# Linear attention and a tanh-shrink MLP on one core: output weights loaded ahead of a query tensor, attention steps moved between matmul slices, activations by pairs of tiles

## The chip, the cores and the metric

One core of a Trainium2 chip. The metric is the device time of one launch in microseconds (us), on the slowest (here the only) core. Executions of this kernel agree within about 0.3%, which is 0.9 us; most runs were repeated and are compared with runs of the kernel before on the same chip in the same rounds.

## The reference

Attention without softmax, by a positive feature map phi, for 8 batches of 576 tokens and 8 heads of 64; its result feeds an MLP over all 4608 tokens. Inputs arrive as float32; the kernel multiplies in bfloat16.

```python
phi  = lambda x: np.where(x > 0, x, np.exp(x) - 1.0) + 1.0
q_p, k_p = phi(q), phi(k)                       # (8, 8, 576, 64)
kv  = np.einsum('bhsd,bhse->bhde', k_p, v)
z   = np.sum(k_p, axis=2)
num = np.einsum('bhsd,bhde->bhse', q_p, kv)
den = np.einsum('bhsd,bhd->bhs', q_p, z)[..., None] + 1e-06
x   = (num / den).transpose(0, 2, 1, 3).reshape(4608, 512)
h   = x @ w_in                                  # w_in  512 x 2048
out = (h - np.tanh(h)) @ w_out                  # w_out 2048 x 512
```

## The kernel before

The tokens go through the MLP in 9 chunks of 512. A chunk is layer 1 (16 tiles of 4 matmuls; each tile is one PSUM bank of 128 x 512, then tanh on ScalarE and a subtraction on VectorE, which writes `gT`) and layer 2 (16 steps of 4 matmuls, then an eviction and a store). A matmul of 512 columns takes 0.216 us at full pace, so a tile or a step takes 0.86 us. The attention of the next batch is put between these matmuls, at places given by the lists `s1` (after a tile of layer 1) and `s2` (after a step of layer 2). As a batch has 576 tokens and a chunk 512, chunk 1 holds the last 64 tokens of batch 0 and the first 448 of batch 1: it can't begin before batch 1's attention is done, and so on.

Chunk 0 is special. Its layer 2 runs while `w_out` is still being loaded, in four slices of 512 KB. So its 16 steps go by slices: steps 0 to 3 use slice 0, steps 4 to 7 slice 1, and so on. Between the steps stand, for batch 1: phi of q, the transposes of q (`a_qT_pe`), kv, the denominator (`a_den`), the numerators with their copy to SBUF by ScalarE (`num1`), and the "spread", a matmul that broadcasts the reciprocals over partitions, after which VectorE multiplies. Numerators and spread use the same four PSUM banks (4 to 7). In the recorded texts, "slice" stands both for a quarter of `w_out` and for what is called a step here.

In the lines of profiles below, PE is TensorE, DVE VectorE, ACT ScalarE, POOL GpSimd, and SPq and ACTq are the DMA issues of SP and ScalarE. TensorE's work has these lines in the kernel before / in the changed one: L367 / L366 layer 1, L382 / L387 layer 2, L165 / L164 transposes of q, L178 / L177 kv of batch 1, L200 / L199 kv of later batches, L277 / L276 denominator, L318 and L321 / L317 and L320 numerators, L355 / L354 spread.

```python
    def l1act(fi, h, gT):
        th = mpool.tile([128, 512], F32, name="th")
        nc.scalar.activation(th, h, AF.Tanh)
        nc.vector.tensor_sub(gT[:, fi, :], h, th)
    ...
    load_q(0); load_k(0); make_identity(nc, ident); load_v(0)
    for g in range(4):
        load_wi(g)
    load_k(1)
    load_wo(0)
    load_q(1)
    ...
    load_wo(1)
    load_v(1)
    load_wo(2)
    ...
            # c == 0
            s2[0].append(lambda: a_qphi(1, 0))
            s2[1].append(lambda: (a_qphi(1, 1), load_q(2), load_wo(3), load_k(2), load_v(2)))
            s2[4].append(lambda: a_qT_pe(1, 0, side))
            s2[5].append(lambda: a_qT_pe(1, 1, side))
            s2[5].append(lambda: (b0_scale_rest(side), prepare()))
            s2[6].append(lambda: a_kv(1, side))
            s2[8].append(lambda: a_den(1, side))
            s2[9].append(lambda: (num1(), a_split(1)))
            s2[11].append(lambda: (spread1(0), a_qphi(2, 0)))
            s2[13].append(lambda: (spread1(1), a_qphi(2, 1), a_qT_dma(2)))
            s2[15].append(lambda: (a_kphi(2, 0), a_vp(2, 0, nc.gpsimd), a_vp(2, 1, nc.gpsimd)))
        elif n1 < B:
            s1[6 if c == 1 else 5].append(lambda: a_kv_cols(n1, attn))
            s1[9 if c == 1 else 8].append(lambda: (a_den(n1, attn), a_spread(n1)))
```

From batch 2 on, `a_spread` broadcasts the reciprocals by DMA instead: four small stores to DRAM (`ds`), then, when these have landed, two loads of 576 KB that read them back to 64 partitions each (`rdb`). All loads are issued by GpSimd; stores and the broadcast by SP.

## Time and profile before

| | kernel before |
|---|---|
| time, median of 3 runs | 295.21 us (295.07 to 295.33) |
| span in the profile | 293.7 us |
| TensorE busy | 285.4 us, 97% |
| VectorE, ScalarE, GpSimd busy | 183.9, 150.6, 34.6 us |
| end of TensorE's last matmul | 289.69 us |

Two more are wanted for the comparison, from the page's groups of instructions of the kernel before (line, engine, operation, operands, shapes, count, then busy us, mean ns of one, then idle us before them and what ended it):

```profile
L373 DVE TENSOR_TENSOR gT<-ps_all,th 128x512 bf16<-128x512 f32 x144 | 96.5, 687 | 46.7 <-ACT th L372 46.0
L372 ACT ACTIVATE th<-ps_all 128x512 f32<-128x512 f32 x144 | 85.3, 597 | 48.1 <-PE ps_all L367 42.2
```

This is the work that the change merges in pairs: 144 subtractions and 144 tanh of one bank each. And the longest of TensorE's waits over the whole kernel before (us in total, times, longest):

```profile
PE ps_all L382 <- DMA w_out_sb<-in_moe_w_out_dram: 1.7, 1, 1.7
```

It is for the second slice of `w_out`, and the one that the change goes for.

### The profile page before, as it was taken

How to read it: one execution, taken by the hardware profiler on the slowest of the kernel's cores; microseconds unless marked ns; L12 is line 12 of the kernel's file. 1: busy time of each engine (PE TensorE's matmuls, PEld its weight loads, DVE VectorE, ACT ScalarE, POOL GpSimd, SP SyncE). 2: the span in 40 equal slices, each digit the busy share in tenths (PEclk: the TensorE clock that was granted, in tenths of full speed). 3: DMA queues.
4: the chain of work that ended last, by engine and by line, in shares of the span. 5: the costliest groups of instructions: out<-in, count | busy, mean ns of one | idle time of the engine just before them, and what ended most of it. 6: DMA issues, size and time to landing. Idle time of an engine off the chain costs nothing.

```text
span 293.7 us, 4685 instructions
## 1 busy us (share of the span) xinstructions
PE 285.4 (97%) x1801; PEld 134.1 (46%) x1801; DVE 183.9 (63%) x326; ACT 150.6 (51%) x233; POOL 34.6 (12%) x55
## 2 busy tenths in 40 slices
PE   8999799999999999999999999999999999999994
PEld 2544364444444444544444445444444444444443
DVE  4759857996578665775578557955780478008600
ACT  4948717766355654555356535752561166136411
POOL 8562030420030002000020003000000000000000
PEclk9999999999999999999999999999999999999998
DMA  7999999897969765957797769787117310130033
GB/s 104 193 205 214 206 206 211 178 186 151 215 119 208 154 142 117 192 120 173 149 152 147 179 138 144 120 203 143 38 34 167 71 37 0 41 85 19 2 71 71
DMA packets 38534, 38.95 MB, mean 133 GB/s; under 512 B 16304, under 2 KB 33264, under 8 KB 37744
## 3 DMA queue, kind: packets, MB, share of 16 engines
q0 software_dynamic: 17008, 18.35, 38.2%
q1 hardware_dynamic: 21424, 20.27, 30.9%
q8 instruction: 14, 0.23, 0.3%
q14 instruction: 8, 0.07, 0.1%
q10 hardware_dynamic: 80, 0.03, 0.0%
HBM read 43.91 MB, written 9.55 MB: 182 GB/s over the span
## 4 chain that ended last, share of the span: by engine, by line
PE 81%; DMA 9%; DVE 5%; POOL 3%; issue 1%; ACT 0%; DVEq 0%; POOLq 0%
PE ps_all L382 39%; PE ps_all L367 35%; DMA w_out_sb<-in_moe_w_out_dram 5%; DMA w_in_sb<-in_moe_w_in_dram 4%; PE ps_all L318 2%; PE ps_all L200 2%; DVE gT L373 1%; PE ps_all L575 1%; DVE xT L360 1%; PE ps_all L277 1%; DVE r L136 1%; DVE kp L137 1%; POOL v L409 1%; PE ps_all L178 1%; DVE qp L137 1%
## 5 line engine op out<-in xcount | busy, mean ns | idle before, releaser
L382 PE MATMUL ps_all<-w_out_sb,gT 128*128 128x512 bf16 x560 | 128.2, 379 | 1.7 <-DMA w_out_sb<-in_moe_w_out_dram 1.7
L367 PE MATMUL ps_all<-xT,w_in_sb 128*128 128x512 bf16 x576 | 128.1, 379 | 0.4 <-DMA w_in_sb<-in_moe_w_in_dram 0.4
L373 DVE TENSOR_TENSOR gT<-ps_all,th 128x512 bf16<-128x512 f32 x144 | 96.5, 687 | 46.7 <-ACT th L372 46.0
L372 ACT ACTIVATE th<-ps_all 128x512 f32<-128x512 f32 x144 | 85.3, 597 | 48.1 <-PE ps_all L367 42.2
L367 PEld LDWEIGHTS <-w_in_sb 128*128 128x128 bf16 x576 | 55.2, 98 | 66.8 <-issue 0.9
L382 PEld LDWEIGHTS <-gT 128*128 128x128 bf16 x560 | 53.9, 98 | 65.9 <-issue 2.1
L388 ACT COPY osb<-ps_all 128x512 f32<-128x512 f32 (+2 forms) x37 | 21.2, 574 | 76.5 <-PE ps_all L382 59.8
L329 DVE TENSOR_TENSOR xT<-ps_all,rdb 128x512 bf16<-128x512 f32 x24 | 16.5, 690 | 14.2 <-PE ps_all L318 14.2
L135 ACT ACTIVATE e<-qraw 128x1152 bf16<-128x1152 bf16 x16 | 18.5, 1163 | 4.6 <-DMA qraw<-in_q_dram 4.6
L137 DVE TENSOR_TENSOR kp<-e,r 128x1152 bf16<-128x1152 bf16 x15 | 12.1, 809 | 12.5 <-ACT e L135 11.6
L135 ACT ACTIVATE e<-kraw 128x1152 bf16<-128x1152 bf16 x15 | 17.4, 1163 | 0.2 <-DMA kraw<-in_k_dram 0.2
L137 DVE TENSOR_TENSOR qp<-e,r 128x1152 bf16<-128x1152 bf16 x16 | 12.1, 758 | 7.9 <-ACT e L135 7.1
L378 POOL COPY g<-gT 1x1 bf16<-1x1 bf16 x5 | 0.9, 179 | 108.4 <-DVE gT L373 108.4
L318 PE MATMUL ps_all<-qT,kz 128*128 128x512 bf16 x28 | 10.1, 379 | 0.0
L434 PE MATMUL ps_all<-zero 128*128 128x512 bf16 x29 | 8.8, 466 | 1.2 <-DVE zero L396 1.2
L136 DVE TENSOR_SCALAR r<-qraw 128x1152 bf16<-128x1152 bf16 x16 | 7.3, 455 | 1.9 <-DMA qraw<-in_q_dram 1.9
L200 PE MATMUL ps_all<-vp,kp 64*128 64x136 bf16 x216 | 7.6, 220 | 0.2 <-DVE kp L137 0.2
L136 DVE TENSOR_SCALAR r<-kraw 128x1152 bf16<-128x1152 bf16 x15 | 7.7, 514 | 0.0
L200 PEld LDWEIGHTS <-kp 64*128 64x128 bf16 x216 | 6.4, 94 | 2.9 <-issue 2.5
L286 DVE RECIPROCAL rden<-den 128x144 f32<-128x144 f32 x7 | 7.4, 1053 | 0.2
L93 POOL DMA_DIRECT2D qraw<-in_q_dram x7 | 5.2, 748 | 14.7 <-DVE r L136 12.3
L93 POOL DMA_DIRECT2D kraw<-in_k_dram x7 | 5.3, 752 | 4.3 <-issue 1.6
(80 smaller groups left out, 105.3 us busy)
## 6 DMA issues: line engine op xcount, KB each, us to landing
out_dram<-osb SPq DMA_DIRECT2D x70, 128.0 KB
rdb<-ds SPq DMA_DIRECT2D x12, 576.0 KB
kraw<-in_k_dram POOLq DMA_DIRECT2D x7, 576.0 KB, 5.9
qraw<-in_q_dram POOLq DMA_DIRECT2D x7, 576.0 KB, 8.0
v<-in_v_dram POOLq DMA_DIRECT2D x7, 576.0 KB, 10.8
w_in_sb<-in_moe_w_in_dram POOLq DMA_DIRECT2D x8, 256.0 KB, 11.7
w_out_sb<-in_moe_w_out_dram POOLq DMA_DIRECT2D x4, 512.0 KB, 14.3
qraw<-in_q_dram POOLq DMA_DIRECT2D x2, 288.0 KB, 4.4
```

The costliest lines, as they stand in the source:

```text
L93: nc.gpsimd.dma_start(out=t.rearrange("q h i j d -> q (h i) (j d)"), in_=x.rearrange("(n q) x -> q n x", n=4))
L135: return (lambda: nc.scalar.activation(e, x, AF.Exp), lambda: nc.vector.tensor_scalar(r, x, 0.0, 1.0, ALU.max, ALU.add), lambda: nc.vector ...
L136: lambda: nc.vector.tensor_scalar(r, x, 0.0, 1.0, ALU.max, ALU.add),
L137: lambda: nc.vector.tensor_tensor(y, e, r, ALU.min))
L200: nc.tensor.matmul(ps[hg][:, i, :], kp[r, i, j].rearrange("p h d -> p (h d)"), vp[r, i, j, :], start=(j == 0), stop=(j == J - 1))
L318: nc.tensor.matmul(ps, kz[:, p // 2, p % 2, 0:128], qT[:, p % 2, 0:8, p // 2, :], start=True, stop=True)
L329: nc.vector.tensor_mul(xT[:, p, S * b:S * b + 512].rearrange("p (j t c) -> p j t c", j=8, t=4), ps.rearrange("p j (t c) -> p j t c", t=4), ...
L367: nc.tensor.matmul(h, w_in_sb[:, 2 * (p % 2) + p // 2, fi * 128:(fi + 1) * 128], xT[:, p, c * 512:(c + 1) * 512], start=(n == 0), stop=(n ...
L372: nc.scalar.activation(th, h, AF.Tanh)
L373: nc.vector.tensor_sub(gT[:, fi, :], h, th)
L382: nc.tensor.matmul(o, gT[:, fi, i * 128:(i + 1) * 128], w_out_sb[:, fi, :], start=(fi == 0), stop=(fi == NF - 1))
L388: nc.scalar.copy(osb[:, f0:f1], o[:, f0:f1])
```

## The change

Its intent: load slice 1 of `w_out` ahead of q of batch 1, and slice 3 ahead of q of batch 2, so that layer 2 of chunk 0 never waits for weights; move what needs q of batch 1 behind step 7; hand the copy `vp` from GpSimd back to VectorE, which it slows; halve the number of activation instructions; spread the last stores over two queues. The core of the diff (cut: the loader of `w_in`, which now takes a size, renamed arguments, and the helper `q2`, whose first and last call a comment stands for):

```diff
-    mpool = ctx.enter_context(tc.tile_pool(name="mpool", bufs=3))
+    mpool = ctx.enter_context(tc.tile_pool(name="mpool", bufs=2))
...
+    def l1act2(fi, h, gT):
+        th = mpool.tile([128, 2, 512], F32, name="th")
+        nc.scalar.activation(th, h, AF.Tanh)
+        nc.vector.tensor_sub(gT[:, fi:fi + 2, :], h, th)
...
-    def gate(gT, fi):
-        nc.gpsimd.tensor_copy(g0, gT[0:1, fi, 0:1])
+    def gate(qT):
+        nc.gpsimd.tensor_copy(g0, qT[0:1, 1, J - 1, 1, 63:64])
...
-        nc.scalar.copy(osb[:, f0:f1], o[:, f0:f1])
+        if f0:
+            nc.vector.tensor_copy(osb[:, f0:f1], o[:, f0:f1])
+        else:
+            nc.scalar.copy(osb[:, f0:f1], o[:, f0:f1])
-        for half, q_ in enumerate((nc.sync, nc.sync if f1 < DM or c < NC - 1 or i < 3 else nc.scalar)):
+        last = c == NC - 1 and i == 3
+        for half in range(2):
-            q_.dma_start(...)
+            (nc.scalar if last and half else nc.sync).dma_start(...)
...
-    for g in range(4):
-        load_wi(g)
+    for f0, n in ((0, 256), (256, 256), (512, 512), (1024, 512), (1536, 512)):
+        load_wi(f0, n)
     load_k(1)
     load_wo(0)
+    load_wo(1)
     load_q(1)
...
-    load_wo(1)
     load_v(1)
     load_wo(2)
+    load_wo(3)
...
-            s2[0].append(lambda: a_qphi(1, 0))
-            s2[1].append(lambda: (a_qphi(1, 1), load_q(2), load_wo(3), load_k(2), load_v(2)))
-            s2[4].append(lambda: a_qT_pe(1, 0, side))
-            s2[5].append(lambda: a_qT_pe(1, 1, side))
-            s2[5].append(lambda: (b0_scale_rest(side), prepare()))
-            s2[6].append(lambda: a_kv(1, side))
-            s2[8].append(lambda: a_den(1, side))
-            s2[9].append(lambda: (num1(), a_split(1)))
-            s2[11].append(lambda: (spread1(0), a_qphi(2, 0)))
-            s2[13].append(lambda: (spread1(1), a_qphi(2, 1), a_qT_dma(2)))
-            s2[15].append(lambda: (a_kphi(2, 0), a_vp(2, 0, nc.gpsimd), a_vp(2, 1, nc.gpsimd)))
+            s2[3].append(lambda: a_qphi(1, 0))
+            s2[4].append(lambda: (a_qphi(1, 1), load_q(2), load_k(2), load_v(2)))
+            s2[0].append(prepare)
+            s2[7].append(lambda: (a_qT_pe(1, 0, side), a_qT_pe(1, 1, side), a_kv(1, side)))
+            s2[8].append(lambda: b0_scale_rest(side))
+            s2[9].append(lambda: a_den(1, side))
+            s2[10].append(lambda: (num1(), a_split(1)))
+            s2[11].append(lambda: spread1(0))
+            # phi of q of batch 2: its exps and maxima after steps 12 and 13, its minima after 14
+            s2[13].append(lambda: (spread1(1), q2(1)))
+            s2[15].append(lambda: a_kphi(2, 0))
         elif n1 < B:
-            s1[6 if c == 1 else 5].append(lambda: a_kv_cols(n1, attn))
-            s1[9 if c == 1 else 8].append(lambda: (a_den(n1, attn), a_spread(n1)))
+            s1[7 if c == 1 else 5].append(lambda: a_kv_cols(n1, attn))
+            s1[10 if c == 1 else 8].append(lambda: (a_den(n1, attn), a_spread(n1)))
         if c == 1:
             s1[1].append(lambda: a_kphi(2, 1))
+            for i in range(2):
+                s1[3].append(lambda i=i: a_vp(2, i))
...
-            l1act(fi, h, gT)
+            if c == 0:
+                l1act(fi, h, gT)
+            elif fi % 2:
+                n = dense.order[(dense.n - 1) % 6]
+                l1act2(fi - 1, ps_all[:, n - 1:n + 1, :], gT)
```

## The prediction

> **What bounds the kernel now.** I read the page first, then the chain of waits in order of time, then the timeline of TensorE over the first 63 us, then those of the other engines, and the landing time of each load. The page has PE busy 97% of a span of 293.7 us. Busy PE is no proof of a full PE, so I looked at the pace in the chain (start us, length us, what):
>
> ```profile
> 21.85 14.25 DMA w_out_sb<-in_moe_w_out_dram
> 36.10 0.04 issue
> 36.14 1.02 PE ps_all L382 x4
> ...
> 67.81 10.36 PE ps_all L382 x48
> ...
> 286.18 3.51 PE ps_all L575 x32
> ```
>
> 48 matmuls of 512 columns in 10.36 us are 0.216 us each, and this pace holds with no other engine in the chain from 62.5 us to 289.7 us. One chunk there (128 such matmuls and the attention ones between) takes 30.36 us (82.61 to 112.96, 112.96 to 143.32, ...). The change removes no matmul. So time can come only from before 62.5 us and from the tail. The timeline of PE shows what is lost there (brackets: idle before, and what ended it):
>
> ```profile
> 30.82 3.62 PE L382 MATMUL ps_all<-w_out_sb,gT 128*128 128x512 bf16 x16
> 36.14 1.02 PE L382 MATMUL ps_all<-w_out_sb,gT 128*128 128x512 bf16 x4 [1.70 <-DMA w_out_sb<-in_moe_w_out_dram]
> ...
> 41.54 1.90 PE L382 MATMUL ps_all<-w_out_sb,gT 128*128 128x512 bf16 x8
> ...
> 44.61 0.28 PE L321 MATMUL ps_all<-qT,kz 128*128 128x64 bf16 x4
> ...
> 47.41 0.30 PE L355 MATMUL ps_all<-w,sel 32*128 32x144 bf16 x8
> ...
> 58.47 0.71 PE L200 MATMUL ps_all<-vp,kp 64*128 64x136 bf16 x18 [0.17 <-DVE kp L137]
> 59.11 2.76 PE L367 MATMUL ps_all<-xT,w_in_sb 128*128 128x512 bf16 x12
> 61.81 0.72 PE L277 MATMUL ps_all<-qT,kz 128*32 128x144 bf16 x16
> 62.46 1.90 PE L367 MATMUL ps_all<-xT,w_in_sb 128*128 128x512 bf16 x8
> ```
>
> The 16 matmuls at 30.82 need 3.45 us, so 36.14 - 34.27 = 1.87 us are lost to the second slice of w_out. In chunk 1, L200 takes 1.5 us instead of 1.17 and L277 0.65 instead of 0.36: some 0.7 us lost to a late VectorE. Two more views matter. ScalarE copies the numerators of batch 1, and VectorE is slow while GpSimd copies vp (52.6 to 55.4):
>
> ```profile
> 44.92 0.37 ACT L347 COPY ns<-ps_all 128x256 f32<-128x256 f32 x1 [5.38 <-PE ps_all L321]
> 45.20 2.06 ACT L345 COPY ns<-ps_all 128x512 f32<-128x512 f32 x4
> ```
> ```profile
> 52.97 1.40 DVE L136 TENSOR_SCALAR r<-kraw 128x1152 bf16<-128x1152 bf16 x1
> 54.48 1.51 DVE L137 TENSOR_TENSOR kp<-e,r 128x1152 bf16<-128x1152 bf16 x1
> ```
>
> The copies end at 47.26, and L355, which writes over all four banks they read, starts at 47.41: already only 0.1 us of slack. The tail is in the DMA queues of SP and ACT:
>
> ```profile
> 290.53 0.55 SPq L392 DMA_DIRECT2D out_dram<-osb  x1
> ```
> ```profile
> 290.01 0.56 ACTq L392 DMA_DIRECT2D out_dram<-osb  x1
> ```
>
> **What the Trainium skill says.** "DMA: Bandwidth & Descriptors", section "Queues, rings and completion order": each DMA engine takes descriptors in ring order, without a promise on completions. The trace agrees with an almost strict queue: issue plus time to landing gives k of batch 1 28.1, w_out slice 0 30.7, q 33.55, slice 1 36.1, v 38.9, slice 2 41.4, then q of batch 2 44.3, slice 3 46.8, k 49.7, v 52.5 us; that is 2.6 us a slice (512 KB) and 2.8 us a tensor (576 KB). "VectorE: DVE Perf Modes", section on the TRN2 errata, gives fp32 tensor_tensor as (N+151)/0.96 ns: 691 for 512 (trace 687), so as an estimate 1224 for 1024. "ScalarE: Activation LUTs", section "What ACT_TABLE_LOAD costs", gives 186 + 0.833 N ns with immediates: 1039 for 1024; the trace's 128x1024 copy took 1012, its 512 tanh 597, so I use 1.02 us. "GPSIMD Engine Reference", section "Specifications": GpSimd shares SBUF interfaces with VectorE in some modes; the two rows above (1.40 for 0.45, 1.51 for two of 0.76) agree.
>
> **Part by part.**
>
> *Order of loads.* w_out slice 1 goes ahead of q of batch 1 and slice 3 ahead of q of batch 2. Same bytes, new places: slice 0 30.7, slice 1 33.3, q 36.1, v 38.9, slice 2 41.4, slice 3 44.0, q of batch 2 46.8, k 49.6, v 52.4. Slices 0 to 7 of layer 2 of chunk 0 then run dense from 30.82 to 37.72: the 1.87 us are gone. But q is 2.55 us later. In the trace before, q at 33.55 gives the first min at 35.50 and the second at 36.74 (landing +1.95, +3.19); so qp comes at 38.05 and 39.3. The transposes (0.5 us each half) now stand right after slice 7: wait 0.4, then 38.65, wait 0.7, done at 39.85. kv (1.59 us) to 41.45. Slice 8 needs w_out slice 2, at 41.4. So slice 8 starts near 41.5. Even with q in time, the landing of slice 2, which the change does not move, would hold it there.
>
> Before, slice 8 began at 42.4, after 0.12 us of L321 that now comes later: so 0.8 us are won at this point. Then: slice 8, L321, slice 9, den (0.36), slice 10: 41.5 + 0.86 + 0.12 + 0.86 + 0.36 + 0.86 = 44.57 for the first numerator (before 44.61, with one slice less behind it). The copies end 2.65 us after it as before, at 47.2. PE has only 0.98 us of numerators and slice 11 (0.86) to fill: it comes to the spread at 46.4 and waits until 47.3. Before: 47.41. **Of 1.87 us won, 0.1 us are left**; the rest has turned into waits for q (1.1) and for ScalarE's copies (0.9).
>
> *Chunk 1.* From 47.3: spread, slices 12 and 13, spread, 14 and 15 bring layer 1 to 51.25 (before 51.45). vp is on VectorE (2 x 0.45), which is no longer slowed by GpSimd (some 1.7 us saved at 53 to 56). Queue on ScalarE: two exps of q, four evictions, exp of k, tanh of the first pair 53.7 to 54.7, exp of k, tanh of the second 55.7 to 56.7. On VectorE: sub of pair one to 56.0, k to 57.2, sub of pair two to 58.35, vp to 58.75 and 59.1. kv now stands one tile later, at 58.16, and waits 0.65 us for vp; it ends at 60.0, three tiles to 62.6, kz is ready at 62.1, den to 62.96 with 44 layer 1 matmuls done. Before it was 62.46 with 40, which is 63.32 with 44. Won: 0.36 us in all.
>
> *Pairs.* 64 pairs for 128 tiles; VectorE saves 64 x (2 x 0.687 - 1.22) = 10 us busy, off the path. The risk is the buffer: a bank was refilled 5 tiles after its own (4.3 us) and freed about 1.4 us after filling; now a pair is refilled after two other pairs (3.45 us) and is free after 0.05 + 1.02 + 0.1 + 1.22 = 2.4 us. Slack 1.05 us. The worst place is den and reciprocal (0.30 + 1.05) ahead of the pair of tiles 8 and 9: from layer 1's start, filled at 10.2, freed at 13.05, wanted at 13.6. The last pair is wanted 3.0 us after its filling and ready after 2.4. So no wait, by 0.5 us.
>
> *Smaller w_in pieces, gate on qT, prepare earlier.* The first layer 1 matmuls waited 0.43 us for w_in, but the next (L241) also waited for VectorE until 16.70. Nothing. The gate moves loads with slack.
>
> *Tail.* Before, SP issues the last three pieces one after the other, the last from 290.53. Now one piece of each pair goes on ACT's queue, and VectorE evicts the last 128 columns. The last issue starts near 290.0: 0.5 us won.
>
> Sum: 0.36 + 0.5 = 0.86 us, so 295.21 to **294.3 us**.
>
> **Rivals.** (1) The stall is really removed: ScalarE's copies or q are no bound, and all 1.87 us are kept with chunk 1's 0.7 and the tail: about 292.1. Against it are the landing of slice 2 at 41.4 and the four banks; for it only that my landings are from one execution. (2) The pairs cost: 0.5 us of wait in each of 7 chunks would bring 297.8. Against it is the slack above; for it that this slack is 0.5 us where it was 2.9. (3) The 512-byte pieces of w_in delay all loads behind them, say by 0.5 us: slice 0, which landed just in time at 30.7, then makes PE wait, and the gain falls to 0.4: 294.8.
>
> **Range and chances.** Rivals 1 and 3 lie around my sum; I take 293.3 to 295.2. 2% is 5.9 us: more than all loss found before 62.5 us and in the tail together (1.87 + 0.7 + 0.5), so faster by 2% has 0.01. Slower by 2% would need 0.9 us in each chunk: 0.01.
>
> **What would show it.** Right: no wait for w_out at slice 4; waits for qp at the transposes (0.4 and 0.7), slice 8 at about 41.5, a wait of about 0.9 us for ScalarE before the first spread at about 47.3, a wait for vp or kp of about 0.6 before kv of chunk 1, chunks of 30.36 us from the second on, last issue near 290.0 minus 0.36. Wrong: the first spread much before 47.3, chunks longer than 30.5 us with PE waiting for the subtraction, or q landing before 35.5.

## The result, and the profile after

The changed kernel took 294.88 us (median of 6 runs, 294.64 to 295.51), the kernel before 295.32 us in the same rounds (6 runs, 295.07 to 295.43). The ratio is 0.9988, with a 95% interval of 0.9975 to 1.0001: the same within 2%, as predicted, and 0.35 to 0.44 us won where 0.86 were predicted. (A ratio here is the mean time of one kernel's runs over that of the other's of the same rounds, so it is not quite the ratio of the medians that are quoted. Executions over 1.5% slower than the fastest of the same kernel are left out of the means.) The interval just includes 1, as does that of a second series of the changed kernel (0.9991, 0.9976 to 1.0006): that anything is won rests on the two series together and on the traces. The profiled spans are 293.7 and 293.2 us.

The loads landed where the model of a strict queue had put them (issue plus time to landing, us):

| load | slice 0 | slice 1 | q, batch 1 | v, batch 1 | slice 2 | slice 3 | q, batch 2 | k, batch 2 | v, batch 2 |
|---|---|---|---|---|---|---|---|---|---|
| predicted | 30.5 to 30.7 | 33.3 | 36.1 | 38.9 | 41.4 | 44.0 | 46.8 | 49.6 | 52.4 |
| found | 30.5 | 33.1 | 35.9 | 38.8 | 41.3 | 43.8 | 46.7 | 49.5 | 52.4 |

The timeline of TensorE in the changed kernel (start us, length us, what, count, and in brackets the idle time before it and what ended it). Matmul ends are modelled and lie some 0.15 us late in a dense stretch, so a bracket understates a wait a little; starts are sure:

```profile
31.03 7.07 PE L387 MATMUL ps_all<-w_out_sb,gT 128*128 128x512 bf16 x32
37.94 0.68 PE L164 MATMUL ps_all<-ident,qp 128*128 128x128 bf16 x9
39.17 0.68 PE L164 MATMUL ps_all<-ident,qp 128*128 128x128 bf16 x9 [0.56 <-DVE qp L136]
...
41.37 1.04 PE L387 MATMUL ps_all<-w_out_sb,gT 128*128 128x512 bf16 x4
...
44.56 0.28 PE L320 MATMUL ps_all<-qT,kz 128*128 128x64 bf16 x4
...
47.26 0.31 PE L354 MATMUL ps_all<-w,sel 32*128 32x144 bf16 x8 [0.69 <-ACT ns L344]
...
51.30 7.07 PE L366 MATMUL ps_all<-xT,w_in_sb 128*128 128x512 bf16 x32
58.74 1.24 PE L199 MATMUL ps_all<-vp,kp 64*128 64x136 bf16 x36 [0.37 <-POOL g L383]
...
62.60 0.43 PE L276 MATMUL ps_all<-qT,kz 128*32 128x144 bf16 x16
```

The first line is what the change wanted: 32 matmuls of layer 2 in a row, over the boundary of slices 0 and 1, with no wait for weights. Step 8 begins at 41.37 instead of 42.4. But between 37.9 and 47.3 stand two new waits, for qp and for ScalarE's copies (`ns`), and the first spread begins at 47.26 instead of 47.41. Of 1.87 us taken away, 0.15 are left at that point.

Set side by side at the same amount of work done (us; the third row is the end of `a_den` with 44 matmuls of layer 1 of chunk 1 done, for the kernel before 62.46 with 40 plus 4 x 0.216):

| TensorE's point | before | predicted | after | won |
|---|---|---|---|---|
| first spread, chunk 0 | 47.41 | 47.3 | 47.26 | 0.15 |
| layer 1 of chunk 1 begins | 51.45 | 51.25 | 51.30 | 0.15 |
| den and 44 matmuls, chunk 1 | 63.32 | 62.96 | 62.97 | 0.35 |
| last matmul ends | 289.69 | 289.33 | 289.36 | 0.33 |
| span ends | 293.7 | 292.84 | 293.2 | 0.5 |

All but the last row came as predicted. From the last matmul to the end of the span the change won 0.2 us (4.01 to 3.82 by the traces' own instants; the sums of rounded lines in the table give 0.17), not 0.5.

These are points of one execution each. In the second profile of the changed kernel (a run of 295.37 us) q landed at 36.17 instead of 35.90, and the points in chunks 0 and 1 all came 0.26 us later: the first spread at 47.52, which is later than before. So an agreement to 0.1 us is partly the luck of this execution; what repeats is which wait stands where.

The chain of waits of the changed kernel has TensorE alone from 63 us on. The starts of layer 1 of two chunks in it:

```profile
112.64 5.18 PE ps_all L366 x24
...
142.99 5.18 PE ps_all L366 x24
```

112.64 to 142.99 is 30.35 us for a chunk, as before (30.36). The groups of the merged activations, to be held against the two lines of before:

```profile
L373 DVE TENSOR_TENSOR gT<-ps_all,th 128x1024 bf16<-128x1024 f32 x64 | 77.9, 1218 | 59.8 <-ACT th L372 59.8
L372 ACT ACTIVATE th<-ps_all 128x1024 f32<-128x1024 f32 x64 | 65.5, 1024 | 57.0 <-PE ps_all L366 47.1
```

1218 and 1024 ns for a pair (1220 and 1020 were estimated) instead of 2 x 687 and 2 x 597. VectorE is busy 174.6 us instead of 183.9 and ScalarE 139.6 instead of 150.6, and the span has nothing of it, since TensorE doesn't wait for them. The waits of TensorE over the whole changed kernel:

```profile
PE ps_all L164 <- DVE qp L136: 0.8, 2, 0.6
PE ps_all L354 <- ACT ns L344: 0.7, 1, 0.7
...
PE ps_all L199 <- POOL g L383: 0.4, 1, 0.4
```

The one wait of 1.7 us for `w_out` has become three smaller ones with a sum of 1.9. From starts alone, the one for qp is 0.73 us (39.17 less 37.94 and 0.50 for nine transposes) and that for the copies 0.86 (47.26 less 45.54 and 0.86 for four matmuls).

### The profile page after: what moved, and what is told of

The parts are those of the page before. It is cut to its first block, busy times and chain, and to the rows that moved or that the text cites. A ratio compares the mean times of both kernels' runs of the same rounds, so it can differ in the third digit from the quotient of the medians.

```text
span 293.2 us, 4504 instructions
## 1 busy us (share of the span) xinstructions
PE 285.2 (97%) x1801; PEld 134.3 (46%) x1801; DVE 174.6 (60%) x265; ACT 139.6 (48%) x168; POOL 33.3 (11%) x55
## 4 chain that ended last, share of the span: by engine, by line
PE 79%; DMA 11%; issue 7%; POOL 2%; DVE 0%; ACT 0%; POOLq 0%
PE ps_all L387 37%; PE ps_all L366 36%; DMA qraw<-in_q_dram 6%; DMA w_in_sb<-in_moe_w_in_dram 3%; PE ps_all L199 2%; DMA kraw<-in_k_dram 2%; PE ps_all L317 2%; PE ps_all L604 1%; PE ps_all L276 1%; POOL qraw L90 0%; ACT e L134 0%; POOL kraw L93 0%; DVE qp L136 0%; POOL v L93 0%; POOL w_out_sb L115 0%
## 5 line engine op out<-in xcount | busy, mean ns | idle before, releaser
L373 DVE TENSOR_TENSOR gT<-ps_all,th 128x1024 bf16<-128x1024 f32 x64 | 77.9, 1218 | 59.8 <-ACT th L372 59.8
L372 ACT ACTIVATE th<-ps_all 128x1024 f32<-128x1024 f32 x64 | 65.5, 1024 | 57.0 <-PE ps_all L366 47.1
L396 ACT COPY osb<-ps_all 128x512 f32<-128x512 f32 (+1 forms) x36 | 20.9, 583 | 73.4 <-PE ps_all L387 54.2
L136 DVE TENSOR_TENSOR kp<-e,r 128x1152 bf16<-128x1152 bf16 x15 | 11.4, 759 | 8.3 <-ACT e L134 7.5
L383 POOL COPY g<-qT 1x1 bf16<-1x1 bf16 x5 | 1.2, 240 | 120.6 <-DMA qT<-qp 120.6
L378 DVE TENSOR_TENSOR gT<-ps_all,th 128x512 bf16<-128x512 f32 x16 | 10.3, 685 | 2.4 <-ACT th L377 1.7
L377 ACT ACTIVATE th<-ps_all 128x512 f32<-128x512 f32 x16 | 9.2, 598 | 4.3 <-PE ps_all L366 3.1
```

The source lines that it names most:

```text
L136: lambda: nc.vector.tensor_tensor(y, e, r, ALU.min))
L373: nc.vector.tensor_sub(gT[:, fi:fi + 2, :], h, th)
L396: nc.scalar.copy(osb[:, f0:f1], o[:, f0:f1])
```

## The experiments

Two theories. **Theory 1**, that of the prediction: the time that slice 1 cost is now spent on waits that stood right behind it (qp, the `ns` copies, `vp` in chunk 1), the other parts of the change are off the path, and the tail gives a little. **The rivals**: the activation pairs or the smaller `w_in` pieces cost what the new order wins; or the bytes on the queue, and not q, hold step 8.

### The order of loads alone

In the kernel before, only the places of the `w_out` loads are changed:

```diff
     load_wo(0)
+    load_wo(1)
     load_q(1)
 ...
-    load_wo(1)
     load_v(1)
     load_wo(2)
+    load_wo(3)
 ...
-  load_q(2), load_wo(3), load_k(2), load_v(2)
+  load_q(2), load_k(2), load_v(2)
```

> The kernel before with the new order of loads alone (w_out slice 1 ahead of q of batch 1, slice 3 ahead of q of batch 2). Theory (what is won at w_out is lost at q): no wait for w_out at slice 4, but q lands at about 35.9 us and the first transposes, still after slice 4, wait 2.5 to 3 us for qp until about 38.0 us, against 37.0 before; all behind them is 0.9 us later; 296.2 us, ratio 1.003. Rival (the 1.87 us wait was simply removable by the order): 293.5 us.

Measured: 297.06 us (4 runs, 296.21 to 297.66) against 295.17; ratio 1.0062 (1.0041 to 1.0084). So by itself the better order of weights loses time. TensorE's timeline shows the wait for qp where the transposes now stand too early:

```profile
37.50 0.68 PE L165 MATMUL ps_all<-ident,qp 128*128 128x128 bf16 x9 [2.18 <-DVE qp L137]
38.22 1.29 PE L382 MATMUL ps_all<-w_out_sb,gT 128*128 128x512 bf16 x3
...
40.50 1.68 PE L382 MATMUL ps_all<-w_out_sb,gT 128*128 128x512 bf16 x4
```

Three matmuls (a fourth has no record) take 1.29 us and four 1.68, where four take 1.04 elsewhere (modelled ends included). The busy time by stretches tells why (stretch, length, busy us and count of PE, PEld, DVE, ACT, POOL, then the granted clock, DMA share, GB/s):

```profile
30.00:37.50 7.50, 5.32 (x26) 2.23 (x24) 4.93 (x10) 4.25 (x6) 0.00 (x0) 1.00 1.22 207
37.50:42.20 4.70, 4.65 (x31) 2.71 (x34) 2.98 (x12) 1.58 (x3) 2.23 (x3) 0.64 1.25 207
42.20:47.00 4.80, 4.64 (x68) 2.91 (x70) 2.54 (x8) 0.00 (x0) 0.00 (x0) 1.00 1.21 208
```

After the idle 2.18 us the granted clock was 0.64 over 4.7 us; in stretches of half a microsecond it was 0.50 in each from 38.5 to 41.5 us, and 1.00 up to 38.0 and from 42.0 on. The mean clock over the span was 0.993 in three of the four runs and 1.0 in the one of 296.21 us, which is the 296.2 that theory 1 expected without any drop. So the wait was foreseen and the drop of the clock was not. The Trainium skill ("TensorE: Matmul & The Clock Gate", Part 1) describes a gate that grants half or all of the pulses by TensorE's activity in windows of about 3.4 us that run free. Half rate for one such window would give, as an estimate from that page, 1 - 0.5 x 3.4 / 4.7 = 0.64 over the stretch: the trace agrees. In the kernels before and after, with single waits of at most 1.9 us, no such drop is seen in chunk 0.

What follows: the moves of the transposes and of kv behind step 7 are a needed part of the change, and the order of loads is worth nothing without them.

### The moves without the order: q first again

In the changed kernel q of batch 1 is loaded ahead of slice 1 again, all else as changed:

```diff
     load_wo(0)
-    load_wo(1)
     load_q(1)
 ...
+    load_wo(1)
     load_v(1)
```

> The changed kernel with q of batch 1 loaded ahead of w_out slice 1 again, all else as changed. Theory: q lands at 33.4, w_out slice 1 at 35.9 us; slice 4 waits 1.5 us for it, no wait at the transposes, slice 8 at about 42.05 instead of 41.37, the first spread at about 47.9; +0.7 us on the changed kernel, 295.6 us. Rival (the order is worth the whole wait it removes): +1.9 us, 296.8. Rival (slice 2 of w_out alone sets the pace): +0, 294.9.

Measured: 295.58 us (4 runs, 295.52 to 295.60), ratio 1.0014 (0.9997 to 1.0030) to the kernel before. The wait for `w_out` is back (0.62 by its bracket where 1.5 was expected, as layer 2 began only at 31.53 here) and that for qp is gone:

```profile
35.77 3.61 PE L387 MATMUL ps_all<-w_out_sb,gT 128*128 128x512 bf16 x15 [0.62 <-DMA w_out_sb<-in_moe_w_out_dram]
39.22 1.17 PE L164 MATMUL ps_all<-ident,qp 128*128 128x128 bf16 x18
...
42.03 1.04 PE L387 MATMUL ps_all<-w_out_sb,gT 128*128 128x512 bf16 x3
...
47.92 0.31 PE L354 MATMUL ps_all<-w,sel 32*128 32x144 bf16 x8 [0.69 <-ACT ns L344]
```

Step 8 at 42.03 and the spread at 47.92 were expected at 42.05 and 47.9. Within the new schedule the order of loads is worth 0.7 us (294.88 against 295.58), and moves without the order would not have beaten the kernel before. The wait for the copies stays at 0.69 in both: it is a fixed distance from the first numerator to the spread (47.92 - 45.22 = 2.70; in the changed kernel 47.26 - 44.56 = 2.70).

### Fewer bytes: slice 1 not loaded at all

Slice 0's rows are used in its place, so the result is wrong (relative error 0.69); everything behind it lands some 2.7 us earlier. This takes away the wait for q without any change of the schedule:

```diff
     load_wo(0)
-    load_wo(1)
 ...
-  nc.tensor.matmul(o, gT[...], w_out_sb[:, fi, :], ...)
+  nc.tensor.matmul(o, gT[...], w_out_sb[:, fi - 4 if 4 <= fi < 8 else fi, :], ...)
```

> The changed kernel without the load of w_out slice 1 (slice 0's rows are used twice, so the result is wrong on purpose). Theory (the landings hold slice 8): every load behind lands 2.5 us earlier (q 33.4, w_out slice 2 38.8), no wait for qp, slice 8 at 40.5 instead of 41.4, spread at 46.4: -0.85 us, 294.0 us. Rival (the wait for ScalarE or another thing would absorb it): 294.9.

Measured: 294.66 us (294.50 to 294.96), ratio 0.9984 (0.9970 to 0.9999). TensorE:

```profile
31.34 7.07 PE L387 MATMUL ps_all<-w_out_sb,gT 128*128 128x512 bf16 x31
38.24 1.17 PE L164 MATMUL ps_all<-ident,qp 128*128 128x128 bf16 x18
...
41.06 1.04 PE L387 MATMUL ps_all<-w_out_sb,gT 128*128 128x512 bf16 x3
...
46.94 0.31 PE L354 MATMUL ps_all<-w,sel 32*128 32x144 bf16 x8 [0.69 <-ACT ns L344]
```

There is no wait between the start of layer 2 and step 8, so TensorE's own work is the bound, and it reaches step 8 at 41.06: only 0.31 us ahead of the changed kernel, since layer 2 began at 31.34 here and at 31.03 there. I had expected 40.5, and 294.0 us in all; the rival, that something else absorbs the gain, was nearer. Three things follow. The landing of q (or of slice 2, which moved with it) is worth 0.3 us as measured and 0.6 from an equal start (41.37 - (41.06 - 0.31)), not more. The wait of 0.69 for the copies is there even when nothing in front of it waits. And the sentence of the prediction that slice 2's landing would hold step 8 anyway was not put to the test by this, as slice 2 landed earlier here too; it stays an argument from the landing at 41.3. In the ten profiles in which slice 1 goes first and the transposes stand behind step 7, kv ends as step 8 begins, and slice 2 landed 0.04 to 0.12 us before that: the two bounds stand at one point, since q and slice 2 come through the same queue, and no run pulls them apart.

The start of layer 2 moved between 30.95 and 31.57 us in the profiles of the changed kernel and its variants. In those that waited for qp it doesn't matter: step 8 came 5.44 to 5.47 us after the first exp of q, at 41.37 for an exp at 35.92 in the changed kernel, at 41.64 for 36.19 in its second profile, and at 41.96 for 36.51 at the most. There, what counts is q's landing (with slice 2's close behind), and that moved by 0.9 us from one profile to another (exps from 35.65 to 36.51). This jitter of the first loads is as large as the effect studied, and is the reason for comparing aligned points and not only ends.

### The numerators one step earlier

```diff
-  s2[9].append(lambda: a_den(1, side))
-  s2[10].append(lambda: (num1(), a_split(1)))
+  s2[9].append(lambda: (a_den(1, side), num1(), a_split(1)))
```

This puts one more layer 2 step between the numerators and the spread, for TensorE to do while ScalarE copies.

> The changed kernel with the numerators of batch 1 after slice 9 instead of after slice 10. Theory (ScalarE's copies of the numerators hold the first spread): numerators at 43.7 instead of 44.6 us, copies end at 46.3 instead of 47.2, the spread then waits only for VectorE's split (about 46.6 us) instead of 47.26: -0.65 us, 294.2 us. Rival (something else sets the spread, such as the split or a landing): spread at 47.2 still, 294.9 us.

Measured: 294.66 us (294.44 to 295.27), ratio 0.9987 (0.9971 to 1.0002). The wait for `ns` is gone and the spread began at 46.54 (46.6 expected, 47.26 in the changed kernel), right after VectorE's split, which ends at 46.49. But of these 0.7 us only 0.2 arrived. The timelines of TensorE and VectorE have a new wait in chunk 1:

```profile
79.63 0.38 PE L317 MATMUL ps_all<-qT,kz 128*128 128x512 bf16 x1 [0.36 <-DVE xT L328]
```
```profile
78.89 1.89 DVE L328 TENSOR_TENSOR xT<-ps_all,rdb 128x512 bf16<-128x512 f32 x3 [2.75 <-DMA rdb<-ds]
```

VectorE waits for the broadcast of batch 2's reciprocals, and the third numerator waits for a bank that VectorE has not read yet. The timeline of VectorE in the kernel before and in the changed one shows where this comes from:

```profile
78.51 0.69 DVE L329 TENSOR_TENSOR xT<-ps_all,rdb 128x512 bf16<-128x512 f32 x1 [1.31 <-PE ps_all L318]
```
```profile
79.10 1.89 DVE L328 TENSOR_TENSOR xT<-ps_all,rdb 128x512 bf16<-128x512 f32 x3 [2.26 <-DMA rdb<-ds]
```

Before, VectorE waited there for TensorE and the broadcast had been in time. In the changed kernel the broadcast comes last, and TensorE loses next to nothing (the third numerator comes 0.04 us late) only because two banks hide the lateness, with nothing to spare. Two shifts met here: the first of these numerators came 0.35 us earlier than before (77.66 for 78.01), and the broadcast was issued 0.29 us later (70.65 for 70.36). So any gain in front of this point runs into it: here the third numerator came 0.5 us late. The prediction had not looked there.

### vp: on GpSimd as before, or earlier on VectorE

First the old engine, in the changed kernel:

```diff
-  s1[3].append(lambda i=i: a_vp(2, i))                       # c == 1, i in 0, 1
+  s2[15]: a_kphi(2, 0), a_vp(2, 0, nc.gpsimd), a_vp(2, 1, nc.gpsimd)   # c == 0
```

> The changed kernel with the copies of vp of batch 2 on GpSimd again. Theory (GpSimd's copies slow VectorE's instructions beside them): VectorE rows of k between 52.4 and 55.5 us take 1.4 instead of 0.45 and near 1.5 instead of 0.76 us in part, so kp comes 0.8 us or more later and kv of chunk 1 waits for kp, 0.2 to 0.7 us. Rival (only where they are queued matters): rows of usual length, kv waits less than the 0.37 us of the changed kernel.

One run, a single look: 295.01 us, state unknown. VectorE and GpSimd side by side:

```profile
52.70 1.40 DVE L135 TENSOR_SCALAR r<-kraw 128x1152 bf16<-128x1152 bf16 x1
54.20 1.51 DVE L136 TENSOR_TENSOR kp<-e,r 128x1152 bf16<-128x1152 bf16 x1
```
```profile
52.44 2.66 POOL L189 COPY vp<-v 128x1152 bf16<-128x1152 bf16 x2 [11.46 <-DMA v<-in_v_dram]
```

The same two VectorE instructions took 0.45 and 0.76 us in the changed kernel. Two copies of some 1.35 us each end near 53.8 and 55.1, and VectorE's two end at 54.10 and 55.71, each some 0.3 to 0.6 us after one of them: as if each had waited for a copy's end and then run (to within 0.15 us of their own lengths). In the kernel before the two end 0.32 and 0.62 us after a copy; and in the run with the order alone two multiplications that read one operand from PSUM (`xT<-ns,ps_all`) took their usual 1.41 us beside the copies. That is what the Trainium skill ("SBUF — State Buffer", section "SBUF: two separate sides") says of the pair of ports that the two engines share, an exclusive lock held for a whole instruction; spans on GpSimd are rough, so this is agreement and no proof. The wait came at another place than I had expected: not at kv, but as 0.28 us for the bank of the next pair, at 56.90. That shows that the slack of the pairs is small in chunk 1, as the prediction had feared, though it held.

Then `vp` on VectorE, but early, while ScalarE still computes the exp that k's phi waits for:

```diff
-  s2[15].append(lambda: a_kphi(2, 0))
+  s2[15]: exp(k), r = max(k, 0) + 1, a_vp(2, 0), a_vp(2, 1), min(e, r)   # in words
-  s1[3].append(lambda i=i: a_vp(2, i))
```

> The changed kernel with VectorE's copies of vp of batch 2 between the two steps of k's first half, at about 53.1 us, in time in which VectorE waited for ScalarE. Theory (kv of chunk 1 waits for vp, not for GpSimd's gate as the profile's name for it says): kv starts 0.37 us earlier, at about 58.35, with no wait. But the broadcast of the reciprocals of batch 2 lands at about 79.0 as before, where the changed kernel has no slack: the third numerator then waits 0.3 us, and the time is 294.8 us, hardly changed. Rival for the wait: kv still starts right after the gate's copy at about 58.7. Rival for the time: 294.5.

Measured: 294.71 us (294.41 to 294.99), ratio 0.9987 (0.9970 to 1.0004). VectorE and TensorE:

```profile
52.99 0.82 DVE L189 COPY vp<-v 128x1152 bf16<-128x1152 bf16 x2
```
```profile
58.20 1.24 PE L199 MATMUL ps_all<-vp,kp 64*128 64x136 bf16 x36
```

The wait of 0.37 us before kv is gone. The changed kernel's waits had named GpSimd's gate (`POOL g L383`) as what ended it; here the gate ran at 58.18, as late as ever, and kv began at 58.20 without a wait. So the name was wrong, and the wait was for `vp`: in the changed kernel VectorE's two copies of it run from 58.23 to 59.05, the first half ends at 58.68, and kv, which begins with that half, starts at 58.74 (in the run without pairs, below: 58.61 and 58.67). From starts the wait was 0.44 us: from the beginning of layer 1 to kv it is 7.44 us in the changed kernel and 7.00 here. The gain of 0.37 showed as less than 0.2 in the time (294.71 against 294.88), partly for the broadcast: the third numerator came 0.18 us later than its place.

### The pairs, and the old tail

The changed kernel with activations tile by tile, and `mpool` with three buffers again:

```diff
-  if c == 0: l1act(fi, h, gT)
-  elif fi % 2: l1act2(fi - 1, ps_all[:, n - 1:n + 1, :], gT)
+  l1act(fi, h, gT)
```

> The changed kernel with layer 1's tanh and subtraction tile by tile again. Theory (VectorE and ScalarE are off the path in the steady part, the pairs cost and win nothing there): chunks from the second on 30.35 us as before, VectorE and ScalarE some 10 us busier; only in chunk 1 kv may wait up to 0.3 us longer for vp; 294.9 to 295.2 us. Rival (the pairs make TensorE wait for banks): faster than the changed kernel by 1 us or more, chunks shorter than 30.3 us. Rival (the pairs win by a lighter VectorE): slower by 1 us or more.

Measured: 294.54 us (294.48 to 294.80), ratio 0.9981 (0.9966 to 0.9996). The changed kernel, run once more on the same chip later, had 294.89 us (5 runs, 294.72 to 295.37; ratio 0.9991, 0.9976 to 1.0006). A chunk takes 30.35 us with either. So pairs neither win nor cost anything that these runs can tell; if anything, they cost 0.1% here, and I had expected equal or slower without them. A part is in the traces: kv of chunk 1 waited 0.25 us for `vp` without pairs and 0.37 with them (`vp` began 6.82 and 6.93 us after layer 1 did), the reverse of what I had expected. The 8 us of VectorE's time that the pairs save (174.6 us busy for 182.9), off the path, are worth nothing.

The changed kernel with all but one of the last stores on SP's queue and ScalarE evicting:

```diff
-  if f0: nc.vector.tensor_copy(osb[:, f0:f1], o[:, f0:f1])
-  else:  nc.scalar.copy(osb[:, f0:f1], o[:, f0:f1])
+  nc.scalar.copy(osb[:, f0:f1], o[:, f0:f1])
-  last = c == NC - 1 and i == 3
+  last = c == NC - 1 and i == 3 and f1 == DM
```

> The changed kernel with the tail of before (last 128 columns copied by ScalarE, one store on ScalarE's queue, three on SyncE's). Theory of the prediction: from TensorE's end to the end of the span 4.0 us again, against 3.5 predicted and 3.84 found in the changed kernel. If the 3.84 are real, the tail gives 0.15 to 0.2 us: 295.05 us. Rival (the 0.17 is noise of the trace): no difference in the tail.

Measured: 295.11 us (294.91 to 295.25), ratio 0.9998 (0.9983 to 1.0013), so 0.2 us slower than the changed kernel by the medians, which alone would be within their scatter. But from the last matmul's end to the end of the span (by the traces' own instants) it has 4.00 us, the kernel before 4.01 and the order alone 4.00, and the changed kernel 3.82 and 3.78 in its two profiles; its nine other variants with the new tail have 3.74 to 3.83. The tail is worth 0.2 us. The timelines of the two queues in the changed kernel say where the rest of the 0.5 went:

```profile
289.70 0.47 SPq L401 DMA_DIRECT2D out_dram<-osb  x1
```
```profile
289.00 1.39 ACTq L401 DMA_DIRECT2D out_dram<-osb  x2
```

The last issue on SP begins at 289.70 (0.34 us after TensorE's end, 0.84 before the change), and ScalarE's queue is at it until 290.39. SP's last issue did come 0.5 us earlier, but after it SP waited 1.6 us for the last landing, before 1.1: the landing didn't follow. What holds it, no run here shows.

### Together, and the broadcast

The numerators and `vp` early, both (the edits of two sections above):

> Numerators of batch 1 one slice earlier and vp earlier. Both waits of chunk 0 and 1 go (0.7 and 0.37 us), but the broadcast of the reciprocals of batch 2 still lands at about 78.9 us, behind the v load of batch 3: the third numerator waits 0.7 to 0.9 us, and of 1.07 us some 0.3 us are left: 294.5 us. Rival (the broadcast moves with the den that starts it): 293.8 us.

Measured: 294.02 us (4 runs, 293.81 to 294.22) against 295.18, ratio 0.9962 (0.9947 to 0.9976). So 0.87 us was won over the changed kernel, where some 0.3 had been expected. By the brackets, TensorE's waits in chunks 0 and 1 are gone but one, which is for a bank that VectorE, late for the broadcast, has not read. (That the wait for qp is gone too is the luck of this profile: layer 2 began late, at 31.40, and q landed early, at 35.63.) The broadcast did move with the den that starts it, as the rival had it: VectorE's first multiplication by it came at 78.29 instead of 79.10. The list of TensorE's waits:

```profile
PE ps_all L317 <- DVE xT L328: 0.4, 1, 0.4
```

The reciprocals are stored from 64.1 us, but the broadcast is issued only when the stores have landed, and the loads of batch 3 were issued just ahead. SP's queue in the changed kernel (the same two steps, 1.3 and 0.8 us later):

```profile
65.45 1.29 SPq L305 DMA_DIRECT2D ds<-rden  x4
70.65 1.12 SPq L308 DMA_DIRECT2D rdb<-ds  x2
```

Four stores of 4.5 KB took until 70.6, which is when v of batch 3 landed (70.67; in the kernel before the two came at 70.36 and 70.37). Two ways to let them past. First, v of batch 3 issued only when the broadcast has landed (a GpSimd copy that reads the last of `rdb` stands ahead of the load):

```diff
-  s1[0]: gate(qT), load_k(n2), load_q(n2), load_v(n2)
+  s1[0]: gate(qT), load_k(n2), load_q(n2)                     # c == 1
+  s1[10]: copy of rdb[64:65, 0, ...] on GpSimd, load_v(n2)    # c == 1, after a_spread
```

> The same, and v of batch 3 is loaded only after the broadcast of the reciprocals of batch 2 has landed. Theory (the broadcast's stores and loads stand behind k, q and v of batch 3 on the same DMA engines): the stores of the reciprocals land with q at about 67.5 instead of 70.5, the broadcast at about 76.3, no wait of the numerators; the whole 1.07 us stays: 293.8 us against 294.9 for the changed kernel. Rival (v comes too late and VectorE waits for it at the end of chunk 1's layer 2): a wait for v at 81 to 83 us that ends in waits of TensorE in chunk 2.

Measured: 295.52 us (6 runs, 293.57 to 297.96), ratio 1.0011 (0.9960 to 1.0063). The broadcast was issued at 68.19 and in by 76.16, and the numerators no longer waited. But v came too late. VectorE and TensorE:

```profile
87.13 0.46 DVE L189 COPY vp<-v 128x1152 bf16<-128x1152 bf16 x1 [5.64 <-DMA v<-in_v_dram]
```
```profile
87.65 1.55 PE L199 MATMUL ps_all<-vp,kp 64*128 64x136 bf16 x36 [0.72 <-DVE vp L189]
```

v was issued at 76.67 and landed near 87, 10.4 us later. The rival came true, and the runs scatter over 4.4 us. One wait had been turned into another.

Second, v issued when the reciprocals are computed (the copy reads `rden`), so that stores and load start together (the diffs here are shortened); in this run the `w_in` pieces are also 512 columns wide again, to test whether the small pieces delay the first loads:

```diff
+  s1[10]: copy of rden[0:1, 0:1] on GpSimd, load_v(n2)        # c == 1
-  for f0, n in ((0, 256), (256, 256), (512, 512), (1024, 512), (1536, 512)):
+  for f0, n in ((0, 512), (512, 512), (1024, 512), (1536, 512)):
```

> The version with numerators and vp early, and v of batch 3 issued when the reciprocals of batch 2 are computed (about 65 us), so behind their stores but not behind the broadcast, as the last run had it; and w_in again in pieces of 512 columns. Theory 1: the stores land with q at about 68 us, the broadcast at 77 to 77.8 instead of 78.3, the numerators wait 0 to 0.1 us instead of 0.4, and v lands near 70.5 us, long before its use: 0.3 to 0.4 us less than 294.0 us, and no slow runs as in the last version. Theory 2 (the smaller pieces of w_in delay the loads of k and v of batch 0, which landed at 8.8 us for k in both kernels with large pieces and at 8.8 to 9.5 in those with small ones): k's exp starts at 8.85 or before and the dense stretch of layer 1 at 17.5; rival: anywhere between 17.4 and 18.2, as with the small pieces. Sum: 293.4 to 293.7 us.

Measured: 293.67 us (5 runs, 293.56 to 294.10) against 295.26, ratio 0.9950 (0.9936 to 0.9963). SP's queue and VectorE:

```profile
68.19 1.12 SPq L308 DMA_DIRECT2D rdb<-ds  x2
```
```profile
77.25 0.69 DVE L328 TENSOR_TENSOR xT<-ps_all,rdb 128x512 bf16<-128x512 f32 x1 [1.23 <-PE ps_all L317]
```

The stores, issued at 64.63, landed 3.6 us later instead of 5.2, the broadcast is in time, the third numerator is no longer late (0.56 us in the version above), and VectorE waits for TensorE again, as in the kernel before. v landed near 72.0, early enough. This version beats the kernel before by 1.6 us and the changed one by 1.2, and in its profile TensorE's only wait between 31 and 290 us is 0.49 us for qp. As two things were changed, and the chip was another one, the 0.35 us from 294.02 are not shown to be v's alone. Theory 2 failed: the first layer 1 stretch began no earlier with the large `w_in` pieces (17.98 us; 17.64 in the changed kernel, 17.43 before). What it follows is the landing of the first half of k of batch 0, 8.6 to 8.8 us ahead of it in all fourteen profiles; that landing moved from 8.74 to 9.49 us, with large pieces 8.74, 8.76 and 9.29. Why, no run shows.

## Why the prediction was right, and where a size was off

- **What bounds the kernel.** Right. Chunks are 30.35 us in both kernels, and all that moved lies ahead of 63 us and behind the last matmul.
- **The order of loads.** Right to a quarter of a microsecond for each of nine loads, and step 8 at 41.37 for 41.5. That 1.87 us of stall would become other waits was right: from starts 0.73 for qp (1.1 predicted; layer 2 began 0.2 us later than before, so the first of its two waits, 0.4 by the prediction, all but fell away), 0.86 for the copies (0.9). The spread came at 47.26 for 47.3; that it came so close is partly luck, as the second profile has 47.52. With slice 1 taken away altogether, and no wait for q left, the spread came at 46.94 only, and still after 0.69 of the same wait.
- **Chunk 1.** Right: 0.36 us won by the end of the denominator predicted, 0.35 found. The wait for `vp` was 0.44 (0.37 by its bracket) and not 0.65, but it stood where predicted, under a wrong name, which an early `vp` unmasked. That the sum fits to 0.01 is luck: 47.3 and the 4.04 us that the next stretch took before make 51.34, where the prediction wrote 51.25, and this nearly cancels the wait that it took too long. (Its 0.7 us lost before in chunk 1 is 0.63 by its own lines.)
- **Pairs.** Right: durations within 4 ns of the estimates, no wait for a bank, no gain. What it had not compared: kv of chunk 1 waits 0.12 us longer for `vp` with pairs than without. The slack is real but small: with VectorE slowed by GpSimd it was overrun by 0.28 us.
- **Small `w_in` pieces, gate, prepare.** No effect was predicted. The large pieces don't start the first stretch earlier. But "the gate moves loads with slack" overlooked what stands behind these loads: those of batch 3 start at 58.9 us instead of 58.1, and the small stores of batch 2's reciprocals wait behind them until 70.65 instead of 70.36. In the changed kernel this costs TensorE nothing yet; it takes part of what further moves win.
- **The tail.** The term that was mis-sized: 0.5 predicted, 0.2 found, by the profiles (3.82 and 3.78 us against 4.01) and by putting the old tail back (295.11 against 294.88). The step "the last issue starts near 290.0: 0.5 us won" took the time of the last issue for that of the last landing. It is some 0.3 of the 0.4 us by which the gain fell short; the rest is within the scatter of the medians.
- **Rivals.** The first (all 1.87 us kept) fell: the banks and q do bind. The second (pairs cost 0.5 us in each chunk) and the third (slice 0 lands late; it came at 30.5) did not show.

Not settled: what sets the landing of the last stores; why q of batch 1 and k of batch 0 land up to 0.9 us earlier or later from one run to the next; and whether slice 2's landing alone would have held step 8 at 41.4.

## What to carry to other kernels

When a stall is taken away, walk on from it with landing times and buffer reuse until the next point that something else fixes, and book only what is left there: here 1.87 us became 0.15 within 10 us of the trace. Reordering the loads paid here only together with moving the consumers of what now comes later; alone it lost 1.9 us (1.0 in the one run without the drop of the clock). Before taking the next gain, look for small stores that must pass large loads. Two small moves of attention steps brought 0.9 us more, twice the gain of the change itself, and took away the slack of such a broadcast; the version that also held one 576 KB load back until the reciprocals were ready was 0.35 us faster still.

## What the Trainium skill lacked or had wrong

- "TensorE: Matmul & The Clock Gate": its rule is to avoid idle gaps of over about 3 us between matmul bursts. A gap of 2.18 us, followed by transposes, brought the granted clock to 0.64 over 4.7 us in the profile, and the mean over the span to 0.993 in three of four runs. The gaps of 1.7 us by brackets in the kernel before had no such effect. The page's Part 4 says that transposes do not count as busy in the same way; counted as idle here, they make the gap some 2.9 us (35.15, which is 30.83 and 20 matmuls of 0.216, to about 38.0), and the rule is nearly met. Whether they count, no run separates.
- "DMA: Bandwidth & Descriptors", section "Queues, rings and completion order": it says that a DMA's completion is signalled only after every earlier write of the same DMA engine, in any queue. The runs agree, and the page has no figure for what this costs small transfers: four stores of 4.5 KB each on SP's queue landed 5.2 us after their first issue when three loads of 576 KB had been issued ahead on GpSimd's, just as the last of these landed, and 3.2 and 3.6 us after it when there were two.
- The same page: a load of 576 KB issued right behind the broadcast took 10.4 us to land, and one issued alongside the small stores 6.8; and issuing the last stores 0.5 us earlier, on two queues, brought the end only 0.2 us forward. No page read here has a figure for these.
- "GPSIMD Engine Reference", section "Specifications": it names the shared interfaces, without a size; the lock that is cited above from "SBUF — State Buffer" would give one. Beside GpSimd's copies of some 1.35 us a tensor_scalar of 128 x 1152 took 1.40 us for 0.45, and a minimum 1.51 for 0.76.
